# Scores, values and transposes of a sparse set issued for both of its units at once

## The chip, the cores and the metric

The kernel runs on one core of one Trainium2 chip. The core has a matrix engine (PE in the profile, with its weight loads listed apart as PEld), a vector engine (DVE), an activation engine (ACT), a general engine (POOL), and a queue processor (SP) that here only issues DMA. Each works through its own instructions in order, and they wait for each other on semaphores. The metric is the device time of one execution in microseconds (us); lower is better. Three runs of the kernel before gave 796.6, 798.16 and 800.87 us.

## The reference

Block-sparse attention over q, k and v of shape 4 batches x 8 heads x 768 positions x 64, then a feed-forward layer, all in float32:

```python
scores = scale * np.matmul(q, k.transpose(0, 1, 3, 2))
# blocks of 32: a query block sees its neighbours, the first and the last
# key block, and 3 sampled blocks; query blocks 0 and 23 see every key
scores = np.where(mask, scores, -1000000000.0)
scores = scores - np.max(scores, axis=-1, keepdims=True)
attn = np.exp(scores)
attn = attn / (np.sum(attn, axis=-1, keepdims=True) + 1e-09)
x = np.matmul(attn, v)                       # then heads are put side by side
h = x @ w_in                                 # 3072 x 512 by 512 x 2048
g = np.maximum(h, 0.0) + np.log1p(np.exp(-np.abs(h)))
out = g @ w_out                              # 3072 x 2048 by 2048 x 512
```

The weights w_in and w_out come as 64-bit floats, which the kernel turns into float32 itself.

## The kernel before, in words

**Attention.** Each batch has 6 groups of 4 query blocks (128 positions). A group makes a sparse set; the sixth group also holds the two query blocks that see all keys, which make a set of their own, called whole, ahead of its sparse remainder (called folded: two query blocks only). So a batch has 7 sets, five ordinary sparse ones, a whole one and a folded one, and the program has 28, numbered from 0. Every set has two units, each half of the heads; unit 2k and 2k+1 belong to set k. What is done for a unit n:

- `scores(n)`: PE multiplies queries and keys into two PSUM tiles `s` (lines 649, 624 and 673 for ordinary, folded and whole sets), and DVE takes scale, mask and row minimum in one pass (655, 629, 680), which empties the tile into `pr`;
- `exponents(n)`: ACT, line 705, from `pr` into `pr`, with the row sums;
- `transposes(n)`: PE, line 718, into PSUM tiles `t`, copied to `pt` by ACT (725) or DVE (723);
- `values(n)`: PE, lines 761, 748 and 775, `pt` times the values `vg`, into the one PSUM tile `x` of the set.

After both units of a set, `normalise` (DVE 788 to 790, tile `xs`), `turn` (PE transposes, 804, into a PSUM tile `y`), `x_high` (ACT 819) and `x_low` (DVE 823) split the result into two float32r parts for the next layer.

**Gathers.** The keys of a sparse set are put together in one of two buffers `kg`: by one DVE copy (516), two ACT copies at the start of a batch (497) and 12 POOL copies (530), from the batch's keys `kT`. The values of a set go into one of two buffers `vg` by DMA from SP (570, 579, 582, 563) and by POOL's indirect DMA (588). `load_keys` and `load_values` put POOL's parts into two lists, and `gather()` takes one entry off each.

**Weights.** The 32 weight halves are converted in stages, one `tick` after another: ACT 160 and 164, DVE 170, 177 and 183, POOL 187, for the early ones also ACT 194 and DVE 201; the others are parked in DRAM.

**Feed-forward.** A loop over j has 48 steps of a first phase (8 tiles of 384 tokens, 6 of 16 slices of the hidden width), then 60 of a second (512 tokens, the other 10 slices). A step issues `hidden` (12 matmuls into a PSUM tile `h`, lines 255 to 257, then ACT 259 and 260), `rounding` (ACT 266, DVE 268 and 269, of which 269 reads `h` last), `logarithm` (ACT 274), `softplus` (DVE 279), `high` (ACT 283), `low` (DVE 289) for the steps before it, and `project` for step j - 3 (9 or 12 matmuls into `o`, 313 to 315). One pool of four PSUM tiles serves `s`, `t`, `y` and `h` in turn.

**What sets the order.** The attention is cut into pieces: a score piece, a value piece and a transpose piece for each n, where the value piece works on unit n, the transposes on n + 1, the scores and exponents on n + 2. After every piece comes one `gather()` and one `convert()` (one tick or half a tick). The pieces of the first sets run before step 0 of the loop; in the loop, `due()` says how many must be done by the middle and the end of each step, so that a token tile's attention is finished before its step needs it. A scheduler then fixes the order of each engine's instructions from this program order; only SP's is left as written. Before the change a step of the loop holds about one unit: scores of one unit, values of another, transposes of a third.

## Time and profile before

| | |
|---|---|
| three runs, us | 796.6, 798.16, 800.87 |
| the profiled execution, us | 799.29, with a span of 797.5 from the first to the last instruction |
| busy share of the span | PE 96%, PEld 76%, DVE 66%, ACT 66%, POOL 27% |
| first loop step starts on PE | 57.08 us |
| last instruction of the attention on PE ends | about 419.7 us |

A row of the timeline has the start, the duration, engine and line, the tile written and those read, the shape, and the number of instructions merged; in brackets stands the idle time before it and what ended it. A matmul's duration is longer than the step to the next one, since they are pipelined; what an instruction costs PE is read from one start to the next. Float32 matmuls are recorded as two instructions, so 16 matmuls of a score unit are x32 there. Lines are those of the kernel before; in the changed kernel the same lines up to `values` and `x_low` stand two further down.

### The profile page before, as it was taken

Reading aid. Unit: us, or ns where it says so; the run is one execution under the profiler, and the core shown is the slowest. Engines: PE = TensorE matmul, PEld = TensorE weight load, DVE = VectorE, ACT = ScalarE, POOL = GpSimd, SP = SyncE. Lnnn points to the kernel's source line nnn. Section 1 sums busy time; section 2 is a strip of 40 time slices with the busy share of each in tenths; the row PEclk is TensorE's granted clock in tenths of the full one; section 3 lists DMA queues with packets and bytes.
Section 4 is the critical chain, followed back from the end, with each engine's and each line's share of the span. In section 5 each row is a group of like instructions: output and inputs, shape, how many; then the busy total and the mean of one; then the engine's idle time right before and its main releaser. Section 6 shows DMA issues by size and latency. Waiting matters only on the chain.

```text
span 797.5 us, 20516 instructions
## 1 busy us (share of the span) xinstructions
PE 768.4 (96%) x7828; PEld 605.4 (76%) x7828; DVE 528.9 (66%) x1231; ACT 528.3 (66%) x1174; POOL 216.4 (27%) x389
## 2 busy tenths in 40 slices
PE   9779989998999999999999999999999999999997
PEld 8556667876777776787788888888888888888886
DVE  6789899787767878785656774555554553644544
ACT  5978978776777776777657875555555555555552
POOL 6874867425455435552000000000000000000000
PEclk9999999998999999999999999999999999999999
DMA  8999997876895886966415940330321312300201
GB/s 248 280 247 316 245 272 206 262 247 204 230 308 180 274 280 175 264 174 208 140 42 186 339 162 1 105 107 1 119 92 37 125 50 95 117 1 2 105 1 53
DMA packets 59729, 129.58 MB, mean 162 GB/s; under 512 B 5552, under 2 KB 17968, under 8 KB 58608
## 3 DMA queue, kind: packets, MB, share of 16 engines
q1 hardware_dynamic: 53632, 109.79, 44.5%
q0 software_dynamic: 5712, 17.57, 7.9%
q8 instruction: 61, 1.00, 0.5%
q10 hardware_dynamic: 288, 0.93, 0.3%
q14 instruction: 36, 0.29, 0.1%
HBM read 97.85 MB, written 30.41 MB: 161 GB/s over the span
## 4 chain that ended last, share of the span: by engine, by line
PE 66%; DVE 16%; ACT 11%; DMA 4%; issue 2%; SPq 0%; ACTq 0%; DVEq 0%
PE o L313 10%; PE o L314 10%; PE o L315 10%; PE h L255 9%; PE h L256 9%; PE h L257 9%; ACT pr L705 4%; PE t L718 2%; DVE pr L655 2%; DVE kg L516 2%; DMA vg<-in_v_dram 2%; PE x L761 2%; PE s L649 2%; DVE e L268 2%; DVE wt L183 1%
## 5 line engine op out<-in xcount | busy, mean ns | idle before, releaser
L268 DVE SCALAR_TENSOR_TENSOR e<-u,e 128x512 f32<-128x512 f32 (+1 forms) x108 | 76.7, 711 | 178.9 <-ACT u L266 178.8
L255 PE MATMUL h<-x,w 128*128 128x512 f32 (+1 forms) x432 | 163.2, 378 | 1.7 <-DVE e L269 0.9
L256 PE MATMUL h<-x,w 128*128 128x512 f32 (+1 forms) x432 | 159.3, 369 | 0.0
L257 PE MATMUL h<-x,w 128*128 128x512 f32 (+1 forms) x432 | 159.1, 368 | 0.0
L313 PE MATMUL o<-w,gh 128*128 128x512 f32 x384 | 156.5, 408 | 0.0
L314 PE MATMUL o<-w,gh 128*128 128x512 f32 x384 | 153.8, 401 | 0.0
L315 PE MATMUL o<-w,gl 128*128 128x512 f32 x384 | 152.1, 396 | 0.0
L259 ACT ACTIVATE e<-h 128x512 f32<-128x512 f32 (+1 forms) x108 | 59.3, 549 | 131.2 <-PE h L257 130.9
L705 ACT ACTIVATE pr<-pr,nmax 128x256 f32<-128x256 f32 (+1 forms) x192 | 102.2, 534 | 24.3 <-DVE nmax L686 12.0
L588 POOL DMA_INDIRECT vg<-in_v_dram,ix x88 | 87.6, 995 | 71.2 <-PE x L761 38.6
L255 PEld LDWEIGHTS h<-x,w 128*128 128x128 f32 x432 | 81.1, 188 | 19.3 <-DVE nmax L680 2.2
L530 POOL COPY kg<-kT 128x128 f32 x252 | 83.8, 378 | 39.4 <-PE s L649 31.2
L313 PEld LDWEIGHTS o<-w,gh 128*128 128x128 f32 x384 | 72.6, 189 | 24.4 <-issue 8.4
L283 ACT CAST gh<-u 128x512 fp32r<-128x512 f32 (+1 forms) x108 | 61.5, 569 | 43.5 <-PE o L314 41.0
L257 PEld LDWEIGHTS h<-x,w 128*128 128x128 f32 x432 | 81.2, 188 | 10.7
L256 PEld LDWEIGHTS h<-x,w 128*128 128x128 f32 x432 | 81.3, 188 | 10.6
L314 PEld LDWEIGHTS o<-w,gh 128*128 128x128 f32 x384 | 72.8, 190 | 17.6 <-issue 2.0
L315 PEld LDWEIGHTS o<-w,gl 128*128 128x128 f32 x384 | 72.6, 189 | 17.6 <-issue 0.4
L274 ACT ACTIVATE u<-u 128x512 f32<-128x512 f32 (+1 forms) x108 | 62.9, 583 | 23.2 <-DVE e L268 22.9
L289 DVE TENSOR_TENSOR gl<-u,gh 128x512 fp32r<-128x512 f32 (+1 forms) x108 | 69.4, 642 | 5.6 <-ACT gh L283 5.6
L279 DVE TENSOR_TENSOR u<-u,e 128x512 f32<-128x512 f32 (+1 forms) x108 | 69.6, 644 | 3.0 <-ACT u L274 1.6
L718 PE MATMUL t<-ident,pr 128*128 128x128 f32 x448 | 63.1, 280 | 7.9 <-DVE x L823 4.8
(88 smaller groups left out, 1060.4 us busy)
## 6 DMA issues: line engine op xcount, KB each, us to landing
vg<-in_v_dram SPq DMA_DIRECT2D x19, 768.0 KB, 6.7
xD<-x SPq DMA_DIRECT2D x8, 1536.0 KB, 8.3
raw<-in_w_in_dram SPq DMA_DIRECT2D x16, 512.0 KB, 9.2
raw<-in_w_out_dram SPq DMA_DIRECT2D x16, 512.0 KB, 8.8
qc<-in_q_dram SPq DMA_DIRECT2D x24, 256.0 KB, 6.9
vg<-in_v_dram SPq DMA_DIRECT2D x12, 512.0 KB, 7.2
yD<-os SPq DMA_DIRECT2D x24, 256.0 KB, 2.4
x<-xD SPq DMA_DIRECT2D x4, 1536.0 KB, 8.6
```

The lines of the kernel that those rows point to most:

```text
L255: nc.tensor.matmul(ph, wh[:, cols], hi[:, c], start=(c == 0), stop=False)
L256: nc.tensor.matmul(ph, wh[:, cols], lo[:, c], start=False, stop=False)
L257: nc.tensor.matmul(ph, wl[:, cols], hi[:, c], start=False, stop=(c == NC - 1))
L268: nc.vector.scalar_tensor_tensor(out=e, in0=u, scalar=-1.0, in1=e, op0=ALU.add, op1=ALU.subtract)
L279: nc.vector.tensor_tensor(out=l, in0=l, in1=e, op=ALU.add)
L313: nc.tensor.matmul(po[m], gh[:, cols], wh, start=first, stop=False)
L314: nc.tensor.matmul(po[m], gh[:, cols], wl, start=False, stop=False)
L315: nc.tensor.matmul(po[m], gl[:, cols], wh, start=False, stop=last)
L530: copy(out=kd[:, i, 1 + NR + s, :], in_=kT[b][:, bass.ds(x, 1), :].rearrange("p n f -> p (n f)"))
L588: nc.gpsimd.indirect_dma_start(out=vd[0 : 3 * BLOCK, 1, i, :], out_offset=None, in_=v, in_offset=bass.IndirectOffsetOnAxis(ap=ix[:, b, 4 * ...
L705: nc.scalar.activation(x, x, AF.Exp, bias=nmax[rows, r, j : j + 1], scale=-1.0, accum_out=rs[rows, h : h + 1])
L718: nc.tensor.transpose(ps[:, i, 0:rows], st["pr"][r][0:rows, c * P : (c + 1) * P], ident[0:rows, 0:rows])
```

## The change

From set 3 on (`SINGLE`) the pieces are no longer made per unit but per set. `set_pieces(k)` gives, for an ordinary sparse set, three pieces: scores of both units of the next set; exponents of both units of the next set with the values of both units of this one; then `normalise`, the transposes of both units of the next set, and `turn`. Whole sets keep their value units apart, with the scores of both units of the set after them in between; ahead of a whole set, the scores of its two units are two pieces. `x_high` and `x_low` of a set move to the front of the next set's first piece. Each piece has a cost, mostly 2: after it, `gather()` and `convert()` run so many times. `due()` counts costs in place of pieces; the sum goes from 174 to 169. The arithmetic and the instructions are the same in kind and number; their order changes.

```diff
--- before.py
+++ after.py
@@ -31,6 +31,8 @@
 WIDE = 4
 
 LEAD = 3
+
+SINGLE = 3
 
 ARRIVAL = 3
 
@@ -873,6 +875,90 @@
         return score_piece, value_piece, transpose_piece
 
 
+    def keys_behind(m):
+        b, g, whole = sets[m]
+        if not whole:
+            load_keys(place[b, g] + 2)
+        elif b + 1 < B:
+
+            gathered(key_work, place[b, g])
+            for n_ in range(4):
+                load_kT(b + 1, n_)
+            load_keys()
+
+    def set_pieces(k):
+
+        last = len(sets) - 1
+        nxt = k + 1 if k < last else None
+        out_ = []
+
+        def scores_first():
+            if k == SINGLE:
+                turn(k - 1)
+                transposes(2 * k + 1)
+            x_high(k - 1)
+            x_low(k - 1)
+            if nxt is not None:
+                scores(2 * nxt)
+                if not sets[nxt][2]:
+                    scores(2 * nxt + 1)
+                    keys_behind(nxt)
+
+        def scores_second():
+            exponents(2 * nxt)
+            scores(2 * nxt + 1)
+            keys_behind(nxt)
+
+        def exponents_next():
+            if nxt is not None:
+                if not sets[nxt][2]:
+                    exponents(2 * nxt)
+                exponents(2 * nxt + 1)
+
+        def behind_values():
+            load_values(k + 2)
+            if nxt is not None and not sets[nxt][2]:
+                load_queries(place[sets[nxt][:2]] + 2)
+
+        def values_first():
+            values(2 * k)
+            transposes(2 * k + 1)
+
+        def values_second():
+            exponents_next()
+            values(2 * k + 1)
+            behind_values()
+
+        def values_both():
+            exponents_next()
+            values(2 * k)
+            values(2 * k + 1)
+            behind_values()
+
+        def transposes_next():
+            normalise(k)
+            if nxt is not None:
+                transposes(2 * nxt)
+                if not sets[nxt][2]:
+                    transposes(2 * nxt + 1)
+            turn(k)
+
+        def split_last():
+            x_high(k)
+            x_low(k)
+
+        if sets[k][2]:
+            out_ += [(1, values_first), (2, scores_first), (1, values_second)]
+        elif nxt is not None and sets[nxt][2]:
+            out_ += [(1, scores_first), (1, scores_second), (2, values_both)]
+        else:
+            out_ += [(2, scores_first), (2, values_both)]
+        out_.append((2, transposes_next))
+        if nxt is None:
+            out_.append((1, split_last))
+        return out_
+
+
 
     early = sorted(((f, which) for f in range(EARLY) for which in range(2)), key=lambda x: (x[0] + LEAD * x[1], x[1]))
     later = [(f, which) for f in range(EARLY, NF) for which in range(2)]
@@ -915,18 +1001,26 @@
     transposes(0)
     exponents(1)
     spread_ends()
-    attention = [piece for n in range(len(units) + 2) for piece in pieces(n)]
-
-    needs = [3 * sum(1 for m, a in units if place[sets[m][:2]] < (t + 1) * GROUPS) + 4 for t in range(NTB)]
-    needs[-1] = len(attention)
+    attention = [(1, piece) for n in range(2 * SINGLE) for piece in pieces(n)]
+    split_in = {m: 3 * (2 * m + 3) + 1 for m in range(SINGLE - 1)}
+    for k_ in range(SINGLE, len(sets)):
+        split_in[k_ - 1] = sum(c for c, _ in attention) + (3 if sets[k_][2] else 2)
+        attention += set_pieces(k_)
+
+    total = sum(c for c, _ in attention)
+    needs = [
+        split_in[max(m for m, x in enumerate(sets) if place[x[:2]] < (t + 1) * GROUPS)] for t in range(NTB - 1)
+    ] + [total]
     done = 0
 
     def attend():
         nonlocal done
-        attention[done]()
-        done += 1
-        gather()
-        convert()
+        cost, piece = attention.pop(0)
+        piece()
+        for _ in range(cost):
+            done += 1
+            gather()
+            convert()
 
     SECOND = NTB * EARLY
     owed = 0.0
@@ -955,7 +1049,7 @@
             if x <= end:
                 return at + (needs[t] - at) * (x - last) / (end - last)
             last, at = end, needs[t]
-        return len(attention)
+        return total
 
     def load_w2(f):
         for which in range(2):
@@ -984,14 +1078,14 @@
             pools["gw"] = ctx.enter_context(tc.tile_pool(name="gw", bufs=2))
             pools["xw", 1] = ctx.enter_context(tc.tile_pool(name="xw1", bufs=1))
         first_half(j)
-        while done < len(attention) and done < due(j + 0.5):
+        while attention and done < due(j + 0.5):
             attend()
         convert()
         second_half(j)
-        while done < len(attention) and done < due(j + 1.0):
+        while attention and done < due(j + 1.0):
             attend()
         convert()
-        if done == len(attention) and ahead is None:
+        if not attention and ahead is None:
             assert weights.done(), weights.at
             actx.close()
             pools["w2"] = ctx.enter_context(tc.tile_pool(name="w2", bufs=1, side="right"))
```

PE, set 16 in the second batch (units 32 and 33; the numbers behind `s`, `t`, `h`, `o` are units and steps, the last number only tells tiles apart). Before, the first row of each run of equal work, from the scores of unit 32 on:

```order
L649 MATMUL s32_0_3989<-kg0_178,qc2_2_3691 32x256
L649 MATMUL s32_1_3990<-kg0_178,qc2_2_3691 32x256
L313 MATMUL o02_0_3594<-w013_1987,gh15_3814 128x512
L804 MATMUL y14_4039<-ident_81,xs14_3943 128x128 x4
L761 MATMUL x30_4045<-vg1_174,pt30_0_3948 32x64 x8
L718 MATMUL t31_0_4080<-ident_81,pr31_0_3851 128x128 x4
L255 MATMUL h19_4099<-x0_3_3098,w001_1101 128x384
L649 MATMUL s33_0_4119<-kg0_178,qc2_2_3691 32x256
L649 MATMUL s33_1_4120<-kg0_178,qc2_2_3691 32x256
L313 MATMUL o02_0_3594<-w014_2087,gh16_3967 128x512
L761 MATMUL x30_4045<-vg1_174,pt31_0_4081 32x64 x8
L718 MATMUL t32_0_4213<-ident_81,pr32_0_3987 128x128 x4
```

The same stretch of PE in the changed kernel:

```order
L651 MATMUL s32_0_4032<-kg0_178,qc2_2_3692 32x256
L651 MATMUL s32_1_4033<-kg0_178,qc2_2_3692 32x256
L651 MATMUL s33_0_4057<-kg0_178,qc2_2_3692 32x256
L651 MATMUL s33_1_4058<-kg0_178,qc2_2_3692 32x256
L257 MATMUL h19_4094<-x0_3_3086,w001_1101 128x384
L315 MATMUL o02_0_3551<-w014_2117,gh16_3950 128x512
L763 MATMUL x30_4135<-vg1_174,pt30_0_3974 32x64 x8
L763 MATMUL x30_4135<-vg1_174,pt31_0_3988 32x64 x8
L257 MATMUL h20_4219<-x0_3_3086,w002_1283 128x384
L720 MATMUL t32_0_4239<-ident_81,pr32_0_4030 128x128 x4
L720 MATMUL t33_0_4253<-ident_81,pr33_0_4055 128x128 x4
L806 MATMUL y15_4267<-ident_81,xs15_4235 128x128 x4
```

The scores of units 32 and 33 now stand side by side, and the step's `h` comes straight behind them, where `o` stood before; both units' values and both units' transposes follow in the same way, each with an `h` or `o` on one side only.

DVE, set 18 (units 36 and 37): the weight steps (`wt`), the split of the set before (`x0` from `y16`), the soft-plus work (`e`, `u`, `gl`) and the reductions (`pr`, one row for each tile). Before:

```order
L170 TENSOR_SCALAR wt112_4554<-wt112_4554 128x512
L268 SCALAR_TENSOR_TENSOR e22_4524<-u22_4559,e22_4524 128x384
L655 ISA pr36_0_4528,nmax36_4527<-s36_0_4530,mask_156 128x256
L655 ISA pr36_1_4529,nmax36_4527<-s36_1_4531,mask_156 128x256
L269 SCALAR_TENSOR_TENSOR e22_4524<-h22_4511,e22_4524 128x384
L177 TENSOR_SCALAR wt112_4554<-wt112_4554 128x512
L279 TENSOR_TENSOR u22_4559<-u22_4559,e22_4524 128x384
L183 SCALAR_TENSOR_TENSOR wt112_4554<-raw112_4015,wt112_4554 128x512
L823 TENSOR_TENSOR x0_4_4044<-y16_4577,x0_4_4044 128x4x128
L289 TENSOR_TENSOR gl21_4683<-u21_4425,gh21_4633 128x384
```

Now:

```order
L270 SCALAR_TENSOR_TENSOR e22_4504<-u22_4551,e22_4504 128x384
L271 SCALAR_TENSOR_TENSOR e22_4504<-h22_4491,e22_4504 128x384
L825 TENSOR_TENSOR x0_4_4006<-y16_4539,x0_4_4006 128x4x128
L172 TENSOR_SCALAR wt112_4618<-wt112_4618 128x512
L179 TENSOR_SCALAR wt112_4618<-wt112_4618 128x512
L291 TENSOR_TENSOR gl21_4642<-u21_4388,gh21_4622 128x384
L281 TENSOR_TENSOR u22_4551<-u22_4551,e22_4504 128x384
L185 SCALAR_TENSOR_TENSOR wt112_4618<-raw112_4083,wt112_4618 128x512
L657 ISA pr36_0_4568,nmax36_4567<-s36_0_4570,mask_156 128x256
L657 ISA pr36_1_4569,nmax36_4567<-s36_1_4571,mask_156 128x256
L657 ISA pr37_0_4593,nmax37_4592<-s37_0_4595,mask_156 128x256
L657 ISA pr37_1_4594,nmax37_4592<-s37_1_4596,mask_156 128x256
```

The reductions of unit 36 stood ahead of the rest of step 22; now they stand behind the split of set 16, `gl21`, `u22` and all three weight steps, and those of unit 37 follow directly.

## Prediction

> **What bounds the kernel now.** I read the busy shares first, then the stages in windows, then PE's timeline in one of them.
>
> ```profile
> PE 768.4 (96%) x7828; PEld 605.4 (76%) x7828; DVE 528.9 (66%) x1231; ACT 528.3 (66%) x1174; POOL 216.4 (27%) x389
> ...
> PEclk9999999998999999999999999999999999999999
> ```
>
> PE is busy nearly all of the span at full granted clock, so PE's own time is what can be won. Where the attention lies beside the loop (up to 419.69 us; behind it the two programs do the same work), the windows give, as columns: the stretch, its length, then busy time and instructions of PE, PEld, DVE, ACT and POOL.
>
> ```profile
> 57.08:168.81 111.73, 105.86 (x1636) 79.69 (x1630) 100.47 (x260) 92.89 (x236) 67.68 (x104) 0.98 0.89 261
> 168.81:278.84 110.03, 105.04 (x1573) 80.54 (x1572) 84.95 (x227) 81.73 (x209) 53.85 (x96) 0.97 0.78 239
> 278.84:382.05 103.21, 100.37 (x1561) 77.30 (x1560) 79.34 (x214) 77.51 (x203) 48.40 (x92) 1.00 0.75 218
> 382.05:419.69 37.64, 37.29 (x502) 29.86 (x501) 21.49 (x60) 22.05 (x50) 1.83 (x2) 1.00 0.27 85
> ```
>
> PE stands idle 5.9, 5.0, 2.8 and 0.3 us in them. DVE is at 90, 77, 77 and 57%: little room in the first batch, some later. Now set 16 on PE, from the scores of unit 32 to those of unit 34:
>
> ```profile
> 230.99 1.09 PE L649 MATMUL s<-kg,qc 64*32 64x256 f32 x32
> 232.02 0.50 PE L313 MATMUL o<-w,gh 128*128 128x512 f32 x1
> 232.36 0.39 PE L314 MATMUL o<-w,gh 128*128 128x512 f32 x1
> 232.59 0.40 PE L315 MATMUL o<-w,gl 128*128 128x512 f32 x1
> ...
> 234.23 0.60 PE L804 MATMUL y<-ident,xs 128*128 128x128 f32 x4
> 234.76 1.10 PE L761 MATMUL x<-vg,pt 128*32 128x64 f32 x64
> 235.79 1.09 PE L718 MATMUL t<-ident,pr 128*128 128x128 f32 x8
> 236.64 0.42 PE L255 MATMUL h<-x,w 128*128 128x384 f32 x1
> 236.90 0.34 PE L256 MATMUL h<-x,w 128*128 128x384 f32 x1
> 237.07 0.34 PE L257 MATMUL h<-x,w 128*128 128x384 f32 x1
> ...
> 238.64 0.34 PE L257 MATMUL h<-x,w 128*128 128x384 f32 x1
> 238.91 1.09 PE L649 MATMUL s<-kg,qc 64*32 64x256 f32 x32
> ...
> 246.38 0.88 PE L649 MATMUL s<-kg,qc 64*32 64x256 f32 x24
> ```
>
> No idle time stands in any row, and still PE loses time. The step between `o` matmuls is 0.23 us, but the first behind the scores takes 0.34; between `h` matmuls it is 0.17, but 0.26 for the first behind the small blocks and 0.27 from the last to the scores. The fourth column shows why: each block with another tile shape (64*32, 128*32, 128*128) starts late and lets the next start late. That is a price per change of shape, and the change moves exactly these.
>
> **The price of a change of shape.** The pure cost of each block comes from places without a change. Behind the attention, `h` and `o` alternate:
>
> ```profile
> 421.88 0.33 PE L255 MATMUL h<-x,w 128*128 128x384 f32 x1
> 423.98 0.40 PE L313 MATMUL o<-w,gh 128*128 128x512 f32 x1
> 426.08 0.34 PE L255 MATMUL h<-x,w 128*128 128x384 f32 x1
> ```
>
> So `h` plus `o` is 4.20 us. Within a score block and a value block, two short windows show where their last rows begin:
>
> ```profile
> 231.45 0.64 PE L649 MATMUL s<-kg,qc 64*32 64x256 f32 x16
> ```
> ```profile
> 235.58 0.28 PE L761 MATMUL x<-vg,pt 128*32 128x64 f32 x5
> ```
>
> The first 16 of 32 score rows took 231.45 - 230.99 = 0.46 us, so 32 take 0.92; the first 59 of 64 value rows took 0.82, so 64 take 0.89. Eight transposes take 0.85 (235.79 to 236.64), the four of `y` half of that, 0.42. The set's period, 246.38 - 230.99 = 15.39 us, holds 2 x (4.20 + 0.92 + 0.89 + 0.85) + 0.42 = 14.14. The rest, 1.25 us, goes to eight changes of shape: **0.16 us each**.
>
> **Part 1: fewer changes of shape.** In the order of PE's instructions from the first `h` on, the shape changes 196 times before and 114 times now; an ordinary set goes from eight to four. 82 x 0.16 = **-13.1 us**. PE's work itself does not change. Of the 362.6 us from 57.08 to 419.69, 196 x 0.16 = 31.4 are such changes, some 300 are pure work (41 `h`, 37 `o` and the attention's rows at the costs above), and 31 are left: idle PE (14.0 in the windows) and starts that were late.
>
> **Part 2: `h` directly behind the scores.** This is the step against the gain. Four PSUM tiles serve `s`, `t`, `y` and `h`. Before, two score tiles were filled and `o`, which needs none of the four, came next: DVE had over 2 us to empty them. Now both units fill all four and `h` comes next, which waits for the reductions of the first. So it is decided by when DVE starts them. Rows of DVE and ACT from the same set:
>
> ```profile
> 233.21 0.42 DVE L655 CUSTOM_DVE_ANT_1 pr<-s,mask 128x256 f32<-128x256 f32 x1
> ...
> 233.55 0.42 DVE L655 CUSTOM_DVE_ANT_1 pr<-s,mask 128x256 f32<-128x256 f32 x1
> ...
> 236.74 0.69 DVE L823 TENSOR_TENSOR x<-y,x 128x512 fp32r<-128x512 f32 x1
> ...
> 244.51 0.41 DVE L177 TENSOR_SCALAR wt<-wt 128x512 int32<-128x512 int32 x1
> 244.85 0.68 DVE L790 TENSOR_TENSOR xs<-x,sums 128x512 f32<-128x512 f32 x1
> 245.45 0.68 DVE L183 SCALAR_TENSOR_TENSOR wt<-raw,wt 128x512 int32<-128x512 int32 x1
> 246.05 0.68 DVE L723 COPY pt<-t 128x512 f32<-128x512 f32 x1
> 246.65 0.55 DVE L279 TENSOR_TENSOR u<-u,e 128x384 f32<-128x384 f32 x1
> 247.11 0.55 DVE L289 TENSOR_TENSOR gl<-u,gh 128x384 fp32r<-128x384 f32 x1
> 247.58 0.16 DVE L788 TENSOR_SCALAR sums<-sums 128x8 f32<-128x8 f32 x1
> ```
> ```profile
> 236.13 0.57 ACT L819 CAST x<-y 128x512 fp32r<-128x512 f32 x1
> ```
>
> Start to start, a reduction costs 0.34, two empty a tile in 0.69; `x_low` costs 0.6, weight steps 0.34, 0.34 and 0.60 (I take 170 like 177), `u` and `gl` 0.46 each. I count from the end of `y` for unit 36, whose order is shown above. PE still has 8 rows of `o` (1.87), then 64 score rows (1.84) and two changes: it wants `h` at 1.87 + 1.84 + 0.2 = 3.9. ACT is through with its copies at about 0.4, `x_high` takes 0.57, `x_low` starts at 1.0 and hands on at 1.6. Then come 0.34 + 0.34 + 0.46 + 0.46 + 0.60 = 2.2, and the first tile is empty at 3.8 + 0.69 + 0.1 = 4.6 to 4.7: **`h` waits 0.75 to 0.85**. Without weight steps there are 0.5 us of slack; with a copy of `o` (0.6) on top it is about 1.4. By DVE's order, of the 16 ordinary sets that follow an ordinary one or start a batch, six have all three weight steps there (one with the copy too), four one or two or a copy, six none. Six cost 0.8 x 5 + 1.4 = 5.4; the four about 2. At a batch's first set the last `h` lies only 5.1 us ahead, and its soft-plus chain on ACT and DVE comes first: 1.1 to 1.75 in each of three, 4.3 together. At three whole sets, whose eight score tiles pass through the same four buffers, I add 1 us each. Sum: **+15 us** of new waits (from 0 if DVE is earlier than walked, to 1.4 in each of 25 sets = 35).
>
> **Part 3: waits that go.** What is late today in ordinary sets is replaced by part 2. Of the 31 us left above I put a third there, **-10** (bounds 5 and 15): the rest lies in the first stage and at the changes of batch, which keep their steps.
>
> **Part 4: gathers and ticks twice a piece** come as often per loop step as before (169 against 174 in all), so the same SP and POOL rows lie in the same places, a set or half a set ahead of their readers. SP waits in order, but for the end of values and scores, as it did. I take 0. The POOL copies behind the scores keep 12 x 0.35 us; were their cover gone, PE would wait up to 4 us a set, which nothing in the order suggests.
>
> Sum: 799.29 - 13.1 + 15 - 10 = **791.2 us**, for the profiled execution. That one was 1.1 above the median of the three runs, so I predict **790** for the median.
>
> **Rivals.** *The reductions are the pace (slower).* If DVE is late in every joined set, since it has no more than a fifth of its time to spare in the two middle stages and a tenth in the first, `h` waits 1.4 us in 25 sets: 35 us, less the 10 that go, against 13.1: 811. It decides from (13.1 + 10) / 25 = 0.9 us a set on. For it: in the walk six sets come near or above that. Against: six sets have slack, and the last stage has no weight work. The Trainium skill, "TensorEngine Tiling (Array Packing)", PSUM Bottleneck, says that tiling speeds up the matrix engine but not the emptying of PSUM, which may then bound; by it this is the case to expect.
>
> *DVE is in time.* The walk stacks ACT's delays pessimistically; if slack of 0.5 us is the rule, the new waits are near 0 and old ones go in part: 798.2 - 13.1 - 5 = 780.
>
> *The gain is lost at the changes of batch.* There POOL makes 18 key copies in a row, and DVE's own key copy beside them took 5.96 us, where its twin takes 1.1:
>
> ```profile
> 187.66 5.96 DVE L516 COPY kg<-kT 128x1536 f32<-128x1536 f32 x1
> ```
> ```profile
> 187.23 4.33 POOL L530 COPY kg<-kT 128x128 f32 x18
> 191.53 1.27 POOL L187 TENSOR_TENSOR wt<-wt,raw 128x512 int32<-128x512 int32 x1
> ```
> ```profile
> 194.27 1.11 PE L718 MATMUL t<-ident,pr 128*128 128x128 f32 x4 [3.19 <-DVE x L823]
> ```
>
> It ended behind POOL's last row, and PE stood 3.2 us. Now this DVE copy stands one set-step earlier, between transposes and `x_low`, and two weight steps behind it could be held as well; some 2.5 us more in each of three changes would leave 797. The Trainium skill, "SBUF — State Buffer", Who interferes with whom, says that such a copy and POOL share a port pair that one holds for a whole instruction while the other is blocked. The trace agrees in kind; that the block lasts through 19 instructions is this row's.
>
> **How the numbers follow.** Forecast 0.47 (790, its own range 784 to 796), DVE in time 0.20 (780), lost at the batches 0.16 (797), reductions the pace 0.17 (811). The measurement can tell about 0.5%, 4 us. Faster (below 794.2): 0.44 + 0.20 = 0.64; the same: 0.03 + 0.15 = 0.18; slower: 0.17 + 0.01 = 0.18. The range for 8 in 10 reaches from 778 to 804: it takes in the zero of part 2 and leaves out the far side of the slow case.
>
> **What would show it.** First `o` and `h` rows behind another shape at 0.34 and 0.26 half as often; ordinary sets without weight steps at 14.7 us a period where 15.4 stood, those with them at 15.5. New idle time of PE `h` (255) put down to DVE's reductions (655), about 10 us, where hardly any stood. The score block of 64 rows at about 1.95 us. I am wrong if this wait is absent or over 25 us, or if a block twice as long costs twice the changes.

## The result, and the profile after

The changed kernel took 808.0 us (median of four runs, 806.73 to 812.03). The kernel before, run again beside it, took 799.21 us. The ratio is 1.0122, with a 95% interval from 1.0075 to 1.0168: **slower by about 1.2%**. The forecast was 790 us, the range ended at 804.

The busy shares and the clock of the page, after the change:

```profile
PE 761.9 (95%) x7828; PEld 610.8 (76%) x7828; DVE 523.4 (65%) x1231; ACT 526.7 (65%) x1174; POOL 218.6 (27%) x389
...
PEclk9998899999999999999999999999999999999999
```

PE's busy time fell by 6.5 us (from 768.4), and the span grew by 8.6 (from 797.5 to 806.1). So PE's idle time rose from 29.1 to 44.2 us. The clock row has lost a tenth in two slices near the start. The new idle time that the prediction named is there, in the group of the first `h` line:

```profile
L257 PE MATMUL h<-x,w 128*128 128x512 f32 (+1 forms) x432 | 163.9, 379 | 12.3 <-DVE nmax L657 11.1
```

To see where the time went, I cut both executions where the first `h` of loop steps 0, 7 and 41 starts: both kernels do the same loop work between these points, and the attention is nearly through at step 41 (of the attention, 64 rows of values have moved behind step 0 and 32 rows of scores ahead of step 7, each some 0.9 us by the costs of the prediction). Each row of this view of windows has the stretch, its length, then busy time and instructions of PE, PEld, DVE, ACT and POOL, then the granted clock. The kernel before:

```profile
0.00:57.08 57.08, 46.47 (x944) 34.45 (x944) 42.11 (x154) 41.86 (x112) 44.63 (x95) 1.00 0.91 256
57.08:128.26 71.18, 65.31 (x991) 47.10 (x985) 67.44 (x171) 60.85 (x152) 46.71 (x73) 0.98 0.99 281
128.26:421.88 293.62, 285.44 (x4287) 222.07 (x4288) 219.59 (x590) 215.06 (x551) 125.04 (x222) 0.99 0.69 209
```

The changed kernel:

```profile
0.00:59.43 59.43, 46.84 (x881) 35.57 (x881) 43.82 (x152) 40.34 (x106) 45.47 (x95) 0.97 0.90 249
59.43:139.36 79.93, 67.47 (x1016) 49.94 (x1017) 69.94 (x174) 61.59 (x155) 46.77 (x73) 0.91 0.84 250
139.36:430.54 291.18, 276.49 (x4319) 223.31 (x4319) 210.28 (x590) 214.35 (x556) 126.34 (x222) 1.00 0.69 209
```

From step 7 to step 41, where three of the four batches lie, the changed kernel is 2.4 us faster. It loses 8.75 us in the first seven steps and 2.35 ahead of them; behind step 41 the two differ by 0.1. **In this execution the loss is made in and ahead of the first batch.** The last column but two shows a part of it: the clock of steps 0 to 7 is 0.91, where 0.98 stood.

Windows of 6 us in which the clock was not full, changed kernel (the first two lie ahead of the loop):

```profile
24.00:30.00 6.00, 3.67 (x93) 2.62 (x78) 3.83 (x13) 5.98 (x19) 5.97 (x22) 0.82 0.77 227
30.00:36.00 6.00, 5.72 (x145) 3.67 (x143) 4.25 (x16) 4.58 (x15) 5.07 (x6) 0.90 0.96 246
...
66.00:72.00 6.00, 4.87 (x26) 1.85 (x26) 5.51 (x14) 3.57 (x7) 2.10 (x2) 0.73 0.93 323
72.00:78.00 6.00, 6.00 (x32) 4.27 (x32) 4.41 (x10) 2.77 (x7) 1.59 (x1) 0.70 0.60 178
90.00:96.00 6.00, 2.76 (x36) 1.46 (x40) 3.52 (x8) 5.99 (x14) 6.00 (x19) 0.72 0.55 152
96.00:102.00 6.00, 6.00 (x66) 5.09 (x59) 6.00 (x16) 3.96 (x11) 4.64 (x9) 0.71 0.61 177
```

The kernel before:

```profile
102.00:108.00 6.00, 3.05 (x40) 1.59 (x38) 6.00 (x9) 2.52 (x6) 5.24 (x6) 0.98 1.06 209
108.00:114.00 6.00, 6.00 (x85) 5.00 (x85) 6.00 (x18) 4.88 (x14) 0.35 (x1) 0.74 1.05 246
192.00:198.00 6.00, 3.73 (x24) 2.29 (x25) 4.87 (x10) 1.19 (x3) 1.76 (x5) 0.59 0.02 8
198.00:204.00 6.00, 6.00 (x68) 5.14 (x68) 2.98 (x7) 4.09 (x10) 2.51 (x5) 0.84 0.50 176
```

Length times the missing share of the clock says what such a spell costs at most (part of it can lie in idle time): 6 x (0.18 + 0.10) = 1.7 us ahead of the loop and 6 x (0.27 + 0.30 + 0.28 + 0.29) = 6.8 in steps 0 to 7 of the changed kernel, against 6 x (0.02 + 0.26) = 1.7 there and 6 x (0.41 + 0.16) = 3.4 at the change of batch in the kernel before. Now the whole difference divides:

| stage | difference, us | PE idle | half clock | the rest of PE's time |
|---|---|---|---|---|
| ahead of step 0 | +2.35 | 10.6 to 12.6: +2.0 | 0 to 1.7: +1.7 | -1.3 |
| steps 0 to 7 | +8.75 | 5.9 to 12.5: +6.6 | 1.7 to 6.8: +5.2 | -3.0 |
| steps 7 to 41 | -2.44 | 8.2 to 14.7: +6.5 | 3.4 to 0: -3.4 | -5.5 |

The last column is what is left over, and holds what the fewer changes of shape brought: 8.5 us from step 0 on (7.1 against a second profile of the kernel before, e5), although 64 rows of values were added there. The idle time ate it, once in the first batch, where it also cost the clock, and once in the later ones.

The waits of PE in steps 0 to 7 of the changed kernel; the one of `h` ended at 59.43 and so lies in the stage ahead of step 0, of whose 2.35 us it is the main part:

```profile
PE s L626 <- POOL kg L532: 4.4, 1, 4.4
PE s L651 <- DVE x L825: 2.9, 2, 1.9
PE h L257 <- DVE nmax L657: 2.2, 1, 2.2
PE t L720 <- ACT pt L727: 1.4, 2, 0.8
```

That `h` waited for the reductions of set 4, which began at 58.52 behind weight steps of DVE. One of these took 1.80 us, where its like in set 18 takes 0.43:

```profile
56.80 1.80 DVE L179 TENSOR_SCALAR wt<-wt 128x512 int32<-128x512 int32 x1
```

The largest wait is put down to POOL's key copies, but those of the folded set were done by 49.6. What the folded set's scores (626) also need are tiles that ACT empties by copying transposes (727), and ACT stood still:

```profile
84.82 0.58 ACT L821 CAST x<-y 128x512 fp32r<-128x512 f32 x1
89.56 0.62 ACT L499 COPY kg<-kT 128x512 f32<-128x512 f32 x1 [4.16 <-DMA kT<-in_k_dram]
...
92.52 0.57 ACT L727 COPY pt<-t 128x512 f32<-128x512 f32 x1
```
```profile
88.44 0.40 PE L316 MATMUL o<-w,gh 128*128 128x512 f32 x1
93.24 0.68 PE L626 MATMUL s<-kg,qc 64*32 64x256 f32 x8 [4.40 <-POOL kg L532]
```

ACT's copy of the new batch's end keys (499) waited for the load of these keys, with the copies of transposes queued behind it; the first of them ended at 93.1, and PE went on at 93.24. This ACT copy is an entry of the list of key gathers, set behind three empty entries so that the load has time. The changed kernel takes two entries after each piece, so the three were used up after a piece and a half.

### The profile page after: what moved, and what is told of

The parts are those of the page before. It is cut to its first block, busy times and chain, and to the rows that moved or that the text cites. A ratio compares the mean times of both kernels' runs of the same rounds, so it can differ in the third digit from the quotient of the medians.

```text
span 806.1 us, 20547 instructions
## 1 busy us (share of the span) xinstructions
PE 761.9 (95%) x7828; PEld 610.8 (76%) x7828; DVE 523.4 (65%) x1231; ACT 526.7 (65%) x1174; POOL 218.6 (27%) x389
## 4 chain that ended last, share of the span: by engine, by line
PE 71%; ACT 9%; DVE 8%; DMA 7%; issue 3%; POOL 1%; SPq 0%; POOLq 0%; DVEq 0%; ACTq 0%
PE h L257 11%; PE h L258 10%; PE h L259 10%; PE o L315 10%; PE o L316 10%; PE o L317 10%; PE x L763 4%; DMA vg<-in_v_dram 3%; ACT pr L707 2%; ACT pt L727 2%; PE s L675 2%; PE t L720 2%; DVE pr L657 1%; DVE wt L185 1%; PE x L777 1%
## 5 line engine op out<-in xcount | busy, mean ns | idle before, releaser
L270 DVE SCALAR_TENSOR_TENSOR e<-u,e 128x512 f32<-128x512 f32 (+1 forms) x108 | 72.7, 673 | 181.7 <-ACT u L268 181.3
L257 PE MATMUL h<-x,w 128*128 128x512 f32 (+1 forms) x432 | 163.9, 379 | 12.3 <-DVE nmax L657 11.1
L261 ACT ACTIVATE e<-h 128x512 f32<-128x512 f32 (+1 forms) x108 | 59.1, 547 | 146.2 <-PE h L259 145.9
L590 POOL DMA_INDIRECT vg<-in_v_dram,ix x88 | 86.2, 979 | 79.9 <-PE x L763 53.9
L532 POOL COPY kg<-kT 128x128 f32 x252 | 86.4, 387 | 29.1 <-PE s L651 24.4
L281 DVE TENSOR_TENSOR u<-u,e 128x512 f32<-128x512 f32 (+1 forms) x108 | 69.2, 640 | 2.6 <-ACT gh L285 0.5
L271 DVE SCALAR_TENSOR_TENSOR e<-h,e 128x512 f32<-128x512 f32 (+1 forms) x108 | 67.9, 629 | 2.6
```

What stands on the lines that cost most here:

```text
L257: nc.tensor.matmul(ph, wh[:, cols], hi[:, c], start=(c == 0), stop=False)
L270: nc.vector.scalar_tensor_tensor(out=e, in0=u, scalar=-1.0, in1=e, op0=ALU.add, op1=ALU.subtract)
L281: nc.vector.tensor_tensor(out=l, in0=l, in1=e, op=ALU.add)
L532: copy(out=kd[:, i, 1 + NR + s, :], in_=kT[b][:, bass.ds(x, 1), :].rearrange("p n f -> p (n f)"))
L590: nc.gpsimd.indirect_dma_start(out=vd[0 : 3 * BLOCK, 1, i, :], out_offset=None, in_=v, in_offset=bass.IndirectOffsetOnAxis(ap=ix[:, b, 4 * ...
```

## The experiments

Seventeen kernels ran, in five series, each beside the kernel before. In two of the series, as with the result, that kernel took 799 to 801 us, in three 811 to 812. Below, "the chip with 800" and "the 811 (or 812) chip" stand for these two cases; that they belong to the chips is not shown, since the record gives chip 9 for a series of each kind (e1 to e4 with 811, e13 to e15 with 800). Ratios are to the kernel before in the same series. Stage times are those of one profiled execution, cut as above.

| kernel | median | ratio, 95% | ahead of 0 | 0 to 7 | 7 to 41 |
|---|---|---|---|---|---|
| before, chip of the result | 799.2 | | 57.1 | 71.2 | 293.6 |
| changed, chip of the result | 808.0 | 1.012 (1.008-1.017) | 59.4 | 79.9 | 291.2 |
| e5 before again | 799.9 | one run | 57.8 | 71.8 | 292.6 |
| e6 changed again | 808.8 | 1.011 (1.007-1.015) | 59.4 | 84.2 | 291.2 |
| e12 changed, 812 chip | 814.1 | 1.004 (1.000-1.007) | 65.6 | 78.9 | 291.1 |
| e1 from set 7, 811 chip | 810.0 | 0.999 (0.996-1.001) | 66.4 | 73.1 | 292.3 |
| e10 from set 7, 812 chip | 811.2 | 0.999 (0.996-1.002) | 68.8 | 72.9 | 291.4 |
| e14 from set 7 | 804.6 | 1.007 (1.004-1.009) | 58.8 | 73.6 | 291.4 |
| e9 from set 4, 812 chip | 813.8 | 1.003 (1.000-1.006) | 66.8 | 74.3 | 291.9 |
| e13 from set 4 | 803.7 | 1.005 (1.003-1.007) | 57.9 | 77.5 | 290.9 |
| e17 from set 9, 811 chip | 813.0 | 1.002 (1.000-1.004) | 69.2 | 70.0 | 296.2 |
| e2 six empty, 811 chip | 812.6 | 1.000 (0.997-1.003) | 65.3 | 79.7 | 291.1 |
| e11 six empty, 812 chip | 812.7 | 1.001 (0.997-1.005) | 63.3 | 76.5 | 295.1 |
| e15 six empty | 804.7 | 1.006 (1.004-1.009) | 59.1 | 76.5 | 290.1 |
| e3 half a step later, 811 chip | 826.2 | 1.018 (1.013-1.023) | 63.5 | 72.7 | 309.3 |
| e4 scores apart, 811 chip | 812.4 | 1.002 (0.999-1.005) | 66.1 | 80.4 | 289.8 |
| e8 apart from set 7 | 799.1 | 0.998 (0.996-1.001) | 57.7 | 72.7 | 290.2 |
| e16 apart from set 9, 811 chip | 810.3 | 0.999 (0.997-1.001) | 68.2 | 71.4 | 294.9 |
| e7 no late weight steps | 809.6 | 1.012 (1.005-1.019) | 59.2 | 81.5 | 289.9 |

### The two kernels again (e5, e6, e12)

No edit; these runs say what differs from one series to another.

> The kernel before, unchanged, for its profile on the chip of this set of runs (the chip of the first four gave it 811 us, the one of the prediction 799). If chips differ in the part ahead of the loop, step 0 starts later than at 57 us and the rest of the span is as long as before; if the loop is slower too, it is not the start.

> The changed kernel, unchanged, on the same chip as the others of this set. If its loss is the first batch's and part of it is a chip's own, the ratio here may differ from the 1.012 of the first chip: theory A (loss belongs to the kernel) 1.008 to 1.017; rival B (a late start of the chip hides it, since set 3 and 4 wait for the same loads anyway) 0.998 to 1.005.

> The changed kernel, unchanged, as the measure for the other three of this set: ratio to the kernel before 1.011 on a chip like the first two; if this is a chip on which the kernel before takes 811 us, 0.998 to 1.003 if the chip's own late start hides the loss, 1.011 if not.

On a second chip with 800 us the loss came again (1.011), with the same 291.2 us from step 7 on and 84.2 in steps 0 to 7. The waits there are much the same as in the first profile, but the clock was at half for 23.9 us in place of 13.7. On the chip with 812 it was 1.004, where 0.998 to 1.003 was expected if the start hides the loss. There the part ahead of the loop took 63 to 69 us in every kernel profiled, and the units (e1, e10) were not earlier at step 0 than the joins (e12): that part seems to hide some of the loss. The kernel before itself has no profile there, so this rests on e1 and e10, whose start is that of the kernel before.

Every execution also has its mean clock on record, and the length times the missing share is the most that half clock can have cost it. In the series of e6 this is 12.5 us in the mean of ten executions of the changed kernel and 7.9 in the mean of nineteen of the kernel before. So up to some 4.7 of the 9.1 us between their means can be half clock.

### Where the loss is made (e1, e10, e14, e9, e13, e17)

```diff
-SINGLE = 3
+SINGLE = 7        # 4 in e9 and e13, 9 in e17
```

> Joins only from set 7 on; the first batch goes in units as in the kernel before. In the traces the changed kernel is 11 us late at loop step 7 and 8.6 us late at the end, so theory A says the loss is made in the first batch's whole and folded sets: about 797 us (795 to 800). Rival B, the joined sets' waits for the reductions set the pace everywhere and the first batch only meets them first: 804 to 808 us.

> Joins from set 7 on, now beside the changed kernel on one chip. The first batch then costs what it cost before, and the later batches gain what they gain in the changed kernel's trace (2.4 us from loop step 7 on): ratio to the kernel before 0.996 to 0.999, to the changed kernel 0.987 to 0.990. If the ordinary joined sets lose too, 1.003 or more.

> Joins from set 7 on, on another chip. Steps 0 to 7 as in the kernel before (71 to 73 us), steps 7 to 41 as in the changed one (291.2): ratio to the kernel before 0.996 to 1.000 on a chip with 800 us. If 1.005 or more, the joined sets of the later batches lose as well.

> Joins from set 4 on: the scores of set 4, ahead of the loop, go in units as before; the whole set 5, the folded set 6 and all later ones as in the changed kernel. In the changed kernel two spells of half clock of 6.8 us each lie in the first batch, one behind the waits around set 4, one behind the folded set's wait. Theory A (each spell follows its own waits): the first goes, the second stays, about half of the loss: ratio to the kernel before 1.004 to 1.007. Rival B (the start is full and any join there pushes the rest): 1.009 to 1.013.

> Joins from set 4 on, on another chip. On the slower chip its loop steps 0 to 7 took 74.3 us against 78.9 of the changed kernel and some 72 of the units. If the joined scores of set 4 ahead of the loop start the loss, that stage takes 73 to 76 us where the changed kernel took 79.9 and 84.2, and the ratio to the kernel before is 1.000 to 1.005 on a chip with 800 us; if the whole and folded sets make it, 1.008 to 1.012.

> The same with the scores joined as in the changed kernel. Later joins gain 2.4 us by the stage from step 7 to 41: ratio 0.996 to 0.999; if a join costs wherever it begins: 1.000 to 1.005.

With the first batch in units, steps 0 to 7 took 72.9 to 73.6 us on both kinds of chip, not 78.9 to 84.2, and the stage behind stayed at 291.4 to 292.3. So in the profiles that stage loses when the first batch is joined. The ratio did not follow all the way: 0.999 on the chips with 811 (to the changed kernel e10 is 0.996, where 0.987 to 0.990 was expected), but 1.0065 on that with 800, where I expected at most 1.000 and wrote that 1.005 or more would mean that the joined sets of the later batches lose as well. The profile does not show where: it is of an execution of 801.6 us, when the ten reach from 800.9 to 808.7 with a median of 804.6. With joins from set 4 on, the part ahead of the loop is that of the kernel before (57.9), steps 0 to 7 took 77.5 and 74.3 (73 to 76 was expected of the first), and of the folded set's wait e13 has 2.4 us, now in front of its transposes, where the changed kernel had 4.4. On the chip with 800 this halves the loss (1.005); e9 is at 1.003, where 1.004 to 1.007 was expected. So about half of it starts with set 4's joined scores ahead of the loop; the other half is there with joins from set 4 and from set 7 on alike, and so is not the first batch's alone. In e17 the first joins lie behind step 7: steps 0 to 7 fell to 70.0, and the stage behind rose to 296.2; the two together are 366.2, against 364.4 and 364.8 in the profiles of the kernel before. **A join seems to cost some 2 us where it begins**; the other expectation, a gain of 2.4 from there on, fell. A part can be seen: the first joined piece holds `turn`, a unit's transposes, `x_low` and the scores of both units in a row, and in e1, e10 and e14 these scores wait 2.0 us for `x_low` (825). In e17 they wait 1.54 us, put down to POOL:

```profile
156.77 1.96 PE L651 MATMUL s<-kg,qc 64*32 64x256 f32 x64 [1.54 <-POOL wt L189]
```

### The keys' load (e2, e11, e15)

```diff
-ARRIVAL = 3
+ARRIVAL = 6
```

> Six empty entries in place of three stand in the list of key gathers at a batch change, so the two ACT copies of a new batch's end keys stand as many pieces behind the load as before, although each piece now takes two entries. Theory A: the 4.4 us that PE waits in front of the first folded set are the ACT copy's wait for that load, passed on by the copies of transposes queued behind it; they go: 803.5 us (802 to 805). Rival B: the wait has another cause (POOL's key copies, as the trace's row names them): 808 us, row still there.

> Six empty gather entries in place of three, beside the changed kernel on one chip. Theory A: the activation engine no longer waits for the keys' load ahead of its transposes' copies, 4.4 us and the spell of half clock behind it go (together up to 7.8): ratio to the changed kernel 0.990 to 0.995. Rival B, from its trace on the other chip, where a wait of 3.7 us for such a copy stood later: the loss only moves, 0.998 to 1.002.

> Six empty gather entries, on another chip. On the slower chip steps 0 to 7 fell from 78.9 to 76.5 us and steps 7 to 41 rose from 291.1 to 295.1: the loss moved. If that holds, the ratio to the kernel before is 1.008 to 1.013 on a chip with 800 us; if the rise was that chip's, 1.003 to 1.007.

The cause of the 4.4 us was the one named: the wait in front of the folded set is gone in all three. But another stands in steps 0 to 7, a few sets later, here in the run on the chip with 800 us:

```profile
PE t L720 <- ACT pt L727: 4.2, 1, 4.2
```

It is again the copies of transposes, late on ACT. ACT came to them at 111.38, behind exponents and weight work and a wait for DVE, and DVE was late from a weight step that ran beside POOL's weight row and key copies:

```profile
101.83 4.33 DVE L179 TENSOR_SCALAR wt<-wt 128x512 int32<-128x512 int32 x1
```

In e2 and e11 such a step takes 3.28 and 3.16 us, where 2.03 is the longest of that line in the changed kernel. So the loss moved in part. Half of it came back on the chip with 800 (1.0064 against 1.011 and 1.012); on the other none can be told: e11 is at 0.998 of the changed kernel, as rival B had it.

### The place of the joined scores (e3, e4, e8, e16)

Half a step later, so that `o` and not `h` follows the joined scores:

```diff
-AHEAD = 0.5
+AHEAD = 0.0
```

> The attention's pieces fall half a step later, so that the joined scores are followed by o, which needs none of the four PSUM tiles, in place of h. Theory A: what costs is the place; h's waits for the reductions (11.1 us in the profile) go: 797 to 800 us. Rival B: joining itself bunches eight reductions and eight exponents, and the wait comes back as t's or s's: 805 to 809 us. By both the matrix engine's busy time stays within 2 us of the changed kernel's 761.9.

This was the worst kernel, above both expectations, and PE's busy time rose to 775.8 us where both had left it within 2 us of 761.9. Steps 7 to 41 took 18 us more than in the changed one, a little of it work that moved behind step 7 (61 more instructions of PE). The window of that stage, then one set on PE:

```profile
136.18:445.44 309.26, 289.70 (x4380) 230.82 (x4380) 212.58 (x597) 223.91 (x559) 128.75 (x224) 0.99 0.65 202
```
```profile
268.76 0.34 PE L259 MATMUL h<-x,w 128*128 128x384 f32 x1
269.03 1.94 PE L651 MATMUL s<-kg,qc 64*32 64x256 f32 x46
272.17 1.07 PE L651 MATMUL s<-kg,qc 64*32 64x256 f32 x18 [1.20 <-DVE nmax L657]
273.16 0.51 PE L315 MATMUL o<-w,gh 128*128 128x512 f32 x1
```

The wait did not go: it moved into the scores. They now follow `h`, which holds one of the four PSUM tiles while the soft-plus work reads it. So only three are left for the scores: the fourth score tile goes into the first one's place and waits for the reductions of that one, where in the changed kernel it was `h` that waited for them. The block of 64 rows took 4.13 us (269.03 to 273.16) in place of 1.95. Two sets of the changed kernel in which `o` follows show the same wait already:

```profile
231.02 1.07 PE L651 MATMUL s<-kg,qc 64*32 64x256 f32 x18 [1.20 <-DVE nmax L657]
```

**Joined scores fill the pool of four**, and whatever stands beside them in that pool waits, in front or behind. These waits are not all of the 18 us: idle time rose by 4.9 and PE's busy time by 13.2, of which half clock is at most 3.4 and the moved scores some 1.8; the rest was not followed.

Scores apart, values and transposes still joined:

```diff
-            if nxt is not None:
-                scores(2 * nxt)
-                if not sets[nxt][2]:
-                    scores(2 * nxt + 1)
-                    keys_behind(nxt)
+            if nxt is not None:
+                scores(2 * nxt)
...
-            out_ += [(2, scores_first), (2, values_both)]
+            out_ += [(1, scores_first), (1, scores_second), (2, values_both)]
```

> Values and transposes stay joined, the two units' scores are separate pieces again, with h between them. Theory A (h right behind joined scores waits): h's waits of 11.1 us fall to 2 or less, PE's busy time rises by some 3 us (27 changes of kind more, about 0.1 us each): 799 to 802 us. Rival B (what is late comes from the transposes and the batch changes): 806 to 809 us.

> Both edits together: first batch in units as before, from set 7 on values and transposes joined with the two units' scores apart. If the first batch's loss and the h waits are two separate losses, this is 3 us below the kernel before (ratio 0.994 to 0.998); if joining values and transposes is worth nothing either, 1.000 to 1.003.

> Units up to set 8, then values and transposes joined and scores apart. If all of the loss is made ahead of step 7 and the later joins gain 3 us as in the run with scores apart from set 7 on: ratio to the kernel before 0.995 to 0.998. If a join costs wherever it begins (the set in which it begins waits): 1.000 to 1.004.

In most ordinary sets PE now has 16 score matmuls, `h`, 16 more; in the first two of the last two batches all 32 still run together, and what is left of the waits stands there. `h`'s waits for the reductions fell from 11.1 us to 2.2 in e4 and 1.9 in e8, and the stage from step 7 to 41 to 289.8 and 290.2: 1.0 to 1.4 us under the changed kernel. Most of what the waits gave was paid back, more than the 3 us that were expected for it: PE's busy time in that stage is 281.5 in e8, 5.0 above the changed kernel's 276.5, of which 32 more rows of scores are some 0.9:

```profile
130.37:420.53 290.16, 281.53 (x4358) 221.49 (x4351) 209.80 (x599) 216.57 (x556) 128.74 (x222) 1.00 0.70 213
```

With the first batch in units, e8 is at 0.998 (0.996 to 1.001): the best of all, and not to be told from the kernel before. Later still (e16) gave 0.999, between its two ranges. No kernel here beat the kernel before beyond its interval.

### The weight steps (e7)

```diff
         def clamp(self, h):
+            if self.halves[h][0] >= EARLY:
+                return
```

and the same in `shift` and for DVE's part of `assemble`.

> The vector engine's three weight steps of the parked halves are left out (the last ten of sixteen slices then hold no converted weights); the matrix engine's order is that of the changed kernel. Theory A of the prediction: the weight steps ahead of the reductions are what makes h wait: its 11 us fall to 4 or less and the kernel to 8 us under the changed one on the same chip, ratio to it 0.990. Rival B: the soft-plus work and the split of the last set are enough to be late: at most 3 us less, ratio 0.996 or more.

The ratio is that of the changed kernel, 1.012. From step 7 to 41 it is 1.3 us faster (289.9 against 291.2), and sets without weight steps ahead of the reductions have nearly no wait left: 0.15 where 0.97 and 1.55 stood. But five others in that stage still wait 0.6 to 1.7, and `h`'s waits come to 8.5 us in all, where 4 or less was expected if the weight steps made them, and 8 or more if not. In one of these sets, DVE waits for ACT's `gh`, which stands behind ACT's own weight work. So the weight steps have a share in `h`'s wait, and not the price of the change.

## Why the prediction was wrong

Three steps failed: the price of a change of shape (part 1), the 10 us of old waits that were to go (part 3), and the start of the program together with the half clock, which the sum held at nothing. The step against the gain (part 2) was right.

**Part 1, fewer changes of shape: right in kind, too large.** It said -13.1 us from step 0 on; the rest of PE's time fell by 8.5. The step that failed is the price of 0.16 us. It divided the excess of a set's period over eight changes of tile shape, but transposes cost at their borders to `h` and `o` too, and these have the same shape. In the changed order such borders are more: one `o` now stands between the transposes. A set without weight steps, on PE:

```profile
377.17 1.47 PE L720 MATMUL t<-ident,pr 128*128 128x128 f32 x12
378.40 0.48 PE L315 MATMUL o<-w,gh 128*128 128x512 f32 x1
378.95 0.66 PE L720 MATMUL t<-ident,pr 128*128 128x128 f32 x4
379.44 0.60 PE L806 MATMUL y<-ident,xs 128*128 128x128 f32 x4
379.80 0.48 PE L316 MATMUL o<-w,gh 128*128 128x512 f32 x1
380.12 0.40 PE L317 MATMUL o<-w,gl 128*128 128x512 f32 x1
```

That `o` costs 378.95 - 378.40 = 0.55 us in place of 0.23. The set's period, from scores to scores, was 15.24 us (366.60 to 381.84), 0.15 of it a wait, where 15.39 stood and 14.7 was forecast. Counted by kind of block (scores, values, transposes, and `h` or `o`), the old set has 11 borders and the new one 8. The excess over the pure 14.14, 1.25 and 0.95, is then 0.11 to 0.12 for each. In the whole order from step 0 on there are 263 such borders before and 188 now, and 75 x 0.114 = 8.5 us is what the rest of PE's time fell by. That agreement is one of sums: by stages, 11 and 65 fewer borders would be 1.3 and 7.4 us, and 3.0 and 5.5 came.

**Part 2, `h` behind the scores: right.** It said +15 us in all. PE's idle time ahead of `h` that DVE's reductions ended was 11.1, with 2.2 of it ahead of step 0. From step 0 on, with scores that waited for the reductions of their own block (651 and 675), such waits are 14.0 us, where 1.8 stood: +12.2. The set that was walked through ran as walked, here DVE and PE of set 18 (first rows of the eight reductions):

```profile
273.77 0.69 DVE L825 TENSOR_TENSOR x<-y,x 128x512 fp32r<-128x512 f32 x1 [0.30 <-ACT x L821]
274.38 0.42 DVE L172 TENSOR_SCALAR wt<-wt 128x512 f32<-128x512 f32 x1
274.83 0.43 DVE L179 TENSOR_SCALAR wt<-wt 128x512 int32<-128x512 int32 x1
275.30 0.56 DVE L291 TENSOR_TENSOR gl<-u,gh 128x384 fp32r<-128x384 f32 x1
275.78 0.55 DVE L281 TENSOR_TENSOR u<-u,e 128x384 f32<-128x384 f32 x1
276.25 0.73 DVE L185 SCALAR_TENSOR_TENSOR wt<-raw,wt 128x512 int32<-128x512 int32 x1
276.85 0.45 DVE L657 CUSTOM_DVE_ANT_1 pr<-s,mask 128x256 f32<-128x256 f32 x1
277.19 0.46 DVE L657 CUSTOM_DVE_ANT_1 pr<-s,mask 128x256 f32<-128x256 f32 x1
```
```profile
274.81 1.96 PE L651 MATMUL s<-kg,qc 64*32 64x256 f32 x64
277.80 0.41 PE L257 MATMUL h<-x,w 128*128 128x384 f32 x1 [1.03 <-DVE nmax L657]
```

0.75 to 0.85 was forecast, 1.03 came; three sets without weight steps waited 0.15 to 0.17. What the Trainium skill, "TensorEngine Tiling (Array Packing)", PSUM Bottleneck, says of emptying PSUM (cited in the prediction) fits these waits and e3, but they were 12 to 14 us and not the 35 of that rival.

**Part 3, waits that go: wrong.** It took 10 us off without a row to rest on, a third of what was left over in a sum. Of these 31 us, 14.0 were idle time and at most 5.1 half clock; the borders of part 1, 263 x 0.114 = 30, come to as much as the 31.4 of the changes of shape, so the rest stays unexplained. From step 0 on, idle time rose by 13.1 us, of which the waits for the reductions are 12.2. All other waits went from 12.2 to 13.1: the -10 came as +0.9. They did fall from step 7 to 41, from 7.6 to 3.0, by the stalls at two changes of batch (3.19 and 1.62 us), which I had said would stay. DVE's key copy that took 5.96 us beside POOL took 2.0 at most in the changed kernel, and the half-clock spell behind that stall went with it. The rival "lost at the changes of batch" had the sign reversed. But steps 0 to 7 got 5.5 us of other waits, with the 4.4 ahead of the folded set.

**What was in no part: the start.** The walk in part 2 covered the sets that follow an ordinary one or begin a batch. By their number, 16, these include only set 4 of the first batch, at 1.4 us or less, and its `h` waited 2.23. The whole set 5 and the folded set 6 were not covered; DVE was at 90% there, and ACT and POOL convert the first weights. Part 4 put the gathers dealt out twice a piece at nothing, since they come as often for a step of the loop. But the empty entries ahead of the key copies count pieces, not steps, and half as many pieces lay between load and copy. The profile shows +2.35 us ahead of the loop and +8.75 in steps 0 to 7, which is more than the whole loss. "Full granted clock" was nearly true of the page's row, which has one 8 among its 9s, and passed over two spells at half clock even before.

The sum with the measured terms, against the span: -8.5 for the borders from step 0 on, +12.2 of waits for the reductions, +0.9 of other waits, +1.7 of half clock (6.8 now, 1.7 and 3.4 before), +2.35 ahead of the loop: +8.65. That this is the 8.6 measured tests nothing, since the -8.5 is what the others leave over; only the 75 borders stand beside it. That the outcome lies near the slow rival's 811 does not confirm that rival: its mechanism came at two fifths of its size, and the stage of the later batches was 2.4 us faster in this profile, not slower. A kernel with joins only in the later batches was not faster for it: 0.999 in e1 and e10, 1.0065 in e14.

What stays open: half clock can be up to some 4.7 of the 9.1 us in the series of e6, but how the rest of the loss follows from single waits cannot be told, since the spells follow the waits; where the 5 us of e14 lie was not profiled; and of what a join costs where it begins (e17) only the wait of 1.5 to 2.0 us in front of its first scores was found.

## What to carry to other kernels

Ask which buffers two joined blocks take up together: where they fill a pool, the next user of that pool can wait, and moving the pair can only move the wait, as in e3. A delay that is counted in pieces, entries or turns changes its length when the pieces change; look for such counters ahead of every load. And walk the start-up of a pipeline by itself: here DVE was at 90% there, against 77% in the stages from which the costs were read.

## What the hardware showed that was not expected

**PE's clock fell to half behind short idle times, and stayed there in units of about 3.4 us.** In the kernel before PE was idle for 2.95 us up to 107.58, and the clock was 0.50 from about 107.7 to 111.2; idle for 3.19 us up to 194.27, half clock from about 193.1 for 6.8 us. In the changed kernel two pieces of idle time, 0.77 us up to 65.90 and 1.13 up to 67.69, were followed by 6.8 us at 0.50 from about 68.8, and the `h` block in that spell took 3.7 us in place of 2.2. A single idle time of 2.23 us ahead of step 0 was followed by none. The Trainium skill, "TensorE: Matmul & The Clock Gate", What's actually happening, gives two states, half clock after an idle window of about 3.4 us and full clock after a busy one, the windows running free. The trace agrees with the two states and the unit of the spells, and with windows that run free: the spells of the changed kernel that begin at 68.75 and 92.65 lie 23.90 us apart, 7.0 times the 3.41 that the shortest lasts. That 1.9 us in two pieces can be enough is this trace's. So a wait in a stage with little slack can cost up to 3.4 us more than it lasts, half of a spell of 6.8 us.

**The same program started later in some series of runs.** Where the kernel before took 811 us, the part ahead of the loop took 66.4 us in the program that is 58.8 in e14. PE's waits name the value matmuls, in e1:

```profile
PE x L763 <- issue: 8.0, 11, 1.9
```

What ended these waits the profile does not name ("issue"); in e5, with 800 us, those of values for their gathers are 0.5 us. Half clock is another part: at most 6.8 us of the 66.4 in e1, 3.4 of the 58.8 in e14. A difference of 1% between two kernels whose start differs can be hidden by that, so they have to be timed side by side, and in more than one series of runs.
